# One transfer for each token tile's store, and single issues for the last pieces

## The chip, the cores and the metric

The kernel runs on one core of a Trainium2 chip. The metric is the device time of one execution in microseconds; the time of a kernel is the median of its runs.

## What is computed

Eight batches, twelve heads, 448 tokens, 64 values per head. Attention has no softmax: the scores are clipped at zero and squared. Its output, 3584 tokens of 768 values, goes through two weight matrices with a clipped square between them.

```python
scores = (q @ k.T) / sqrt(64)              # per batch and head, 448 x 448
attn   = maximum(scores, 0) ** 2 / 448
x      = (attn @ v), heads side by side    # 3584 x 768
h      = x @ w_in                          # 3584 x 2048
g      = maximum(h, 0) ** 2
out    = g @ w_out                         # 3584 x 768, float32
```

## The kernel before

Work goes by pairs of batches, `pr` = 0 to 3. For each pair there is a stage that forms g (batches 0 and 1 with plain products, line 430; later ones with a Strassen scheme, line 559) and then an output stage that forms `out` (line 746, seven half products for two token tiles, a Strassen scheme again). The attention of later batches is woven into both stages in `visit`s (lines 263 to 273, 329, 388).

**Token tiles.** The 448 tokens of a batch are laid out as 64 partitions times J = 7, token = 7p + j. A token tile of the output has 128 rows, that is two values of j with 64 partitions each; a pair of batches has seven such tiles, `tb` = 0 to 6. Tile 3 takes j = 6 of the first batch and j = 0 of the second; every other tile lies in one batch.

**Groups.** An output stage is a list of groups, each of two token tiles: `groups` in `o_steps`. Even pairs have three groups and save their tile 6; odd pairs have four, with the saved tile in the second. The last group of all is `LAST`, tiles 5 and 6 of pair 3. Within a group the products run in the order end1, end2, end6, end5, end7, end4, end3, each named for what happens after it: `end2` allocates the two output tiles `osb` and writes the first half row of the first of them (VectorE, line 653), `end4` finishes the second tile (ScalarE, line 696) and stores it, `end3` finishes the first tile (VectorE, line 653) and stores it. The first product of the next group is placed ahead of end4's.

**Output tiles.** `osb0` and `osb1` have two buffers each (pool "osb", 2). A buffer is written again two groups later, after its store has landed.

**Stores and queues.** `store` (lines 577 to 585) issues two transfers for each token tile, one for each j, from 64 partitions each. SyncE issues them. SyncE also issues the DMA transposes that turn q and k for the attention units to come (line 120); a unit's transposes are issued about two units ahead of its use. GpSimd issues the loads (lines 95 to 144); those of q and k for a later unit (line 109) reuse a buffer that the transposes read, and so wait for them.

**The last group** stores in pieces: two half rows on SyncE (end2, end7), a half row on GpSimd (end4), and the last half row in two quarters (`end3_part`), of which SyncE issues the first j and ScalarE the second:

```python
plus(0, c, "u5", acc=W, cc=cc)
store(rows[0], osb[0], c, nc.sync, nc.scalar)
```

Of the kernel before, what the change touches and what calls it, by code (L numbers as in the profile page):

```python
# [18 lines left out]
def kernel(  # L19
# [9 lines left out]
    nc = tc.nc  # L29

    B, H, S, D = q.shape
# [12 lines left out]
    J = 7  # L44
# [529 lines left out]
        return [(0.096, step(p, r, m), r == 0 and m == 0 and p not in (0, 1, 6, 8))  # L574
                for p in range(14) for r in range(2) for m in range(NH)]

    def store(row, osb, c, eng, eng2=None):
        pr, tb = row
        for i in range(2):
            b, j = divmod(2 * tb + i, J)  # L580
            b += 2 * pr
            (eng2 if eng2 and i else eng).dma_start(  # L582
                out=out[b * S:(b + 1) * S, :].rearrange(
                    "(p j) d -> p j d", j=J)[:, j, c],
                in_=osb[64 * i:64 * i + 64, c])
# [31 lines left out]
    def o_groups(groups, then):  # L617
# [5 lines left out]
        def group(n, rows, last):  # L623
# [3 lines left out]
            c0, c1 = slice(0, HALF), slice(HALF, DM)  # L627
# [8 lines left out]
            def ahead(i, k=n):  # L636
                if k < len(groups) and i not in sets[k]:
                    flush_g(needs(k))
                    sums(i, groups[k], sets[k])
# [11 lines left out]
            def plus(row, c, nm, acc=Y, cc=slice(0, HALF)):  # L651
                now_ve(0.5)
                nc.vector.scalar_tensor_tensor(  # L653
                    out=osb[row][:, c], in0=acc[0][:, 0:cc.stop - cc.start], scalar=CO,
                    in1=keep[nm][:, cc], op0=ALU.mult, op1=ALU.add)
# [8 lines left out]
            def end2():  # L664
                new_osb()
                plus(0, c0, "m1")
                if last:
                    store(rows[0], osb[0], c0, nc.sync)
# [8 lines left out]
            def end7():  # L677
                copy("u3")
                plus(1, c1, "u3")
                if last:  # L680
                    store(rows[1], osb[1], c1, nc.sync)
                    t = late["m"].tile([P, S], FP32, name="u5", tag="a")[:, 0:HALF]
                    nc.vector.scalar_tensor_tensor(
                        out=t, in0=Y[0][:, 0:HALF], scalar=CO, in1=keep["u2"],
                        op0=ALU.mult, op1=ALU.add)
                    keep["u5"] = t
# [4 lines left out]
            def end4():  # L691
                if last:
                    plus(1, c0, "u3", acc=Z)
                    store(rows[1], osb[1], c0, nc.gpsimd)
                    return
                nc.scalar.activation(out=osb[1][:, c0], in_=X[0][:, 0:HALF],
                                     func=AF.Copy, scale=CO)
                store(rows[1], osb[1], slice(0, DM), nc.sync)
                ahead(1, n + 1)
                ahead(2, n + 1)  # L700
# [5 lines left out]
            def end3_part(z):  # L706
                h = HALF // 2
                cc = slice(z * h, z * h + h)
                c = slice(HALF + cc.start, HALF + cc.stop)
                plus(0, c, "u5", acc=W, cc=cc)  # L710
                store(rows[0], osb[0], c, nc.sync, nc.scalar)

            products = (
                (X, True, lambda: tile_of(rows[0])[:, LO], b11, end1),
# [2 lines left out]
                (Y, True, lambda: ss[1], t1, end5),  # L717
                (X, False, lambda: ss[3], t3, end7),
                (X, False, lambda: tile_of(rows[1])[:, HI], nt4, end4),
                (Y, False, lambda: ss[4], b22, end3))  # L720

            def step3(z, f):
                h = HALF // 2

                def run():
                    if f == 0:
                        W[:] = [mm_tile(z)]
                    nc.tensor.matmul(
                        W[0][:, 0:h], lhsT=ss[4][:, f], rhs=b22[:, f, z * h:z * h + h],
                        start=(f == 0), stop=(f == KH - 1))  # L730
                    if f == KH - 1:
                        end3_part(z)
                return run
# [313 lines left out]
```

## Time and profile before

| | |
|---|---|
| median of 3 runs | 369.84 us (369.5 to 369.86) |
| the profiled execution | 369.71 us |
| its span | 367.9 us, granted TensorE clock 0.999 |
| busy share of the span | PE 98%, VectorE 72%, ScalarE 68%, GpSimd 29% |
| DMA | 42.65 MB moved, mean 116 GB/s |
| stores of 192 KB (SyncE) | 52, median 3.3 us from issue to landing |
| stores of the last group | 10: six of 96 KB and four of 48 KB, medians 2.2 to 2.9 us |

PE is TensorE's matmuls, DVE is VectorE, ACT ScalarE, POOL GpSimd, SP SyncE; a "q" behind a name is that engine's sequencer. The output stages lie at about 78 to 119, 162 to 212, 253 to 290 and 326 to 363 us of the span. Loads end at about 300 us; after that only stores move.

### The profile page before, as it was taken

The numbers are of one execution on the slowest core, as the hardware profiler recorded it, in microseconds if no ns is written. First come the engines' busy times: TensorE is split into PE (matmuls) and PEld (weight loads), VectorE is DVE, ScalarE is ACT, GpSimd is POOL, SyncE is SP. The second block draws the span as 40 slices with busy tenths as digits, with TensorE's granted clock in tenths as the row PEclk, the third lists the DMA queues.
The fourth block names the chain that finished last, engine by engine and source line by source line (L and its number), as shares of the span: only waits on it lengthen the run. The fifth ranks groups of instructions, "written<-read, shape, count | busy, mean of one in ns | idle before, by whom it ended". The sixth has DMA issues, their size and how long they took to land.

```text
span 367.9 us, 8740 instructions
## 1 busy us (share of the span) xinstructions
PE 358.8 (98%) x3588; PEld 232.1 (63%) x3588; DVE 265.3 (72%) x470; ACT 248.6 (68%) x384; POOL 107.2 (29%) x128
## 2 busy tenths in 40 slices
PE   8899999999999999999999999999999999999994
PEld 3644445445556788875555687886555689976662
DVE  2997677987867679888575667788876687784442
ACT  3988895788676998877655678886766785532220
POOL 8635521856552254531045225320000000000001
PEclk9999999999999999999999999999999999999999
DMA  8999999999999999967799998992323300003333
GB/s 119 196 204 203 205 204 161 144 160 166 207 124 155 170 111 134 99 92 61 138 146 125 156 159 83 107 90 52 67 71 87 86 3 2 2 0 87 86 96 78
DMA packets 121160, 42.65 MB, mean 116 GB/s; under 512 B 100832, under 2 KB 117760, under 8 KB 121120
## 3 DMA queue, kind: packets, MB, share of 16 engines
q0 software_dynamic: 82912, 23.01, 61.7%
q1 hardware_dynamic: 38048, 18.98, 26.5%
q8 instruction: 28, 0.46, 0.5%
q10 hardware_dynamic: 160, 0.10, 0.1%
q14 instruction: 12, 0.10, 0.1%
HBM read 45.61 MB, written 11.01 MB: 154 GB/s over the span
## 4 chain that ended last, share of the span: by engine, by line
PE 89%; DVE 4%; ACT 3%; issue 2%; DMA 1%; POOL 0%; POOLq 0%; ACTq 0%
PE mm L746 33%; PE mm L559 27%; PE mm L430 9%; PE slot L263 9%; PE slot L329 7%; ACT at L273 2%; DVE at L388 1%; DMA k<-in_k_dram 1%; DVE at L304 1%; PE mm L263 1%; PE avt L287 1%; PE slot L238 1%; ACT xt L342 1%; PE mm L238 0%; DVE osb L653 0%
## 5 line engine op out<-in xcount | busy, mean ns | idle before, releaser
L273 ACT ACTIVATE at<-slot 128x896 f16<-128x896 f32 x156 | 135.5, 927 | 7.4 <-PE slot L263 7.4
L388 DVE TENSOR_TENSOR at<-at 128x896 f16<-128x896 f16 x147 | 86.7, 618 | 12.6 <-ACT at L273 11.9
L109 POOL DMA_DIRECT2D qs<-in_q_dram x36 | 35.3, 983 | 111.1 <-DMA qT<-qs 102.8
L746 PEld LDWEIGHTS <-s 128*128 128x128 f16 x440 | 41.8, 98 | 32.2 <-issue 4.8
L559 PEld LDWEIGHTS <-w 128*128 128x128 f16 x576 | 53.8, 98 | 6.8 <-issue 6.0
L263 PE MATMUL slot<-qT,kT 64*64 64x448 f16 x696 | 53.2, 359 | 1.9 <-ACT at L273 1.4
L559 PE MATMUL mm<-xt,w 128*128 128x224 f16 x432 | 49.2, 259 | 0.0
L746 PEld LDWEIGHTS <-g 128*128 128x128 f16 x336 | 31.9, 98 | 23.5 <-issue 3.8
L559 PEld LDWEIGHTS <-ws 128*128 128x128 f16 x432 | 40.8, 98 | 2.8 <-issue 2.8
L746 PE MATMUL mm<-b,g 128*128 128x384 f16 x224 | 40.7, 326 | 0.0
L430 PE MATMUL mm<-xt,w 128*128 128x448 f16 x192 | 39.8, 354 | 0.0
L746 PE MATMUL mm<-b,s 128*128 128x384 f16 x216 | 39.5, 326 | 0.0
L746 PE MATMUL mm<-t,s 128*128 128x384 f16 x224 | 38.8, 326 | 0.0
L109 POOL DMA_DIRECT2D ks<-in_k_dram x36 | 35.2, 979 | 9.6 <-DMA b<-in_moe_w_out_dram 5.8
L263 PEld LDWEIGHTS <-kT 64*64 64x64 f16 x744 | 20.3, 104 | 27.6 <-issue 21.5
L653 DVE SCALAR_TENSOR_TENSOR osb<-mm,u 128x384 f32<-128x384 f32 (+1 forms) x30 | 16.2, 541 | 28.4 <-ACT u L648 20.9
L582 POOL DMA_DIRECT2D out_dram<-osb x2 | 1.1, 563 | 120.9 <-DVE osb L653 120.9
L502 DVE CUSTOM_DVE_ANT_0 g<-mm,m 128x448 f16<-128x448 f32 x36 | 22.4, 621 | 18.4 <-PE mm L559 7.8
L648 ACT ACTIVATE u<-mm 128x384 f32<-128x384 f32 x28 | 14.2, 507 | 30.5 <-PE mm L746 28.4
L559 PE MATMUL mm<-x,ws 128*128 128x224 f16 x288 | 33.7, 259 | 0.0
L329 PE MATMUL slot<-at,vt 64*64 64x448 f16 x560 | 30.1, 349 | 0.0
L430 PEld LDWEIGHTS <-w 128*128 128x128 f16 x192 | 17.1, 98 | 19.2 <-issue 5.1
(80 smaller groups left out, 417.2 us busy)
## 6 DMA issues: line engine op xcount, KB each, us to landing
out_dram<-osb SPq DMA_DIRECT2D x52, 192.0 KB, 3.3
vt<-in_v_dram POOLq DMA_DIRECT2D x24, 224.0 KB, 6.8
qs<-in_q_dram POOLq DMA_DIRECT2D x36, 112.0 KB, 4.9
ks<-in_k_dram POOLq DMA_DIRECT2D x36, 112.0 KB, 5.8
w<-in_moe_w_in_dram POOLq DMA_DIRECT2D x8, 384.0 KB, 12.1
b<-in_moe_w_out_dram POOLq DMA_DIRECT2D x4, 768.0 KB, 17.1
q<-in_q_dram POOLq DMA_DIRECT2D x6, 224.0 KB, 7.2
k<-in_k_dram POOLq DMA_DIRECT2D x6, 224.0 KB, 7.7
```

The source lines that it names most:

```text
L109: nc.gpsimd.dma_start(out=t[:, :, hh, :], in_=heads(src, n)[:, hh].rearrange("p (j d) -> p j d", d=D))
L238: nc.tensor.transpose(pss[i][64 * hh:64 * hh + 64, i if n < 4 else 0, j * P:(j + 1) * P], src[:, hh, j * D:(j + 1) * D], ident)
L263: nc.tensor.matmul(ps[hh][c, 0:S] if spare else ps[c, hh, 0:S], lhsT=kT[r, j, c], rhs=qT[r, :, c], start=True, stop=True)
L273: nc.scalar.activation(out=at, in_=ps[:, :, 0:S], func=AF.Relu, scale=SK)
L329: nc.tensor.matmul(ps[hp][64 * hh:64 * hh + 64, 0:S] if spare else ps[64 * hh:64 * hh + 64, hp, 0:S], lhsT=vt[r, hh, j * D:(j + 1) * D], r ...
L388: lambda: nc.vector.tensor_mul(at, at, at), 0))
L430: nc.tensor.matmul(cell[0][:, 0:S], lhsT=w1[f // 4][:, m, (f % 4) * P:(f % 4 + 1) * P], rhs=xts[b][:, m, :], start=(m == 0), stop=(m == NM ...
L502: nc.vector._custom_dve(TENSOR_ADD_SAT, out=gs(s, hi, right), in0=acc(s, y), in1=keep[s, nm], s0=3.4e38, s1=0.0)
L559: nc.tensor.matmul(XY[s][y][:, r * Q:(r + 1) * Q], lhsT=left(k, i0 + 2 * s + r, m), rhs=right(k, m), start=(fresh and r == 0 and m == 0), ...
L648: nc.scalar.activation(out=t, in_=X[0][:, 0:HALF], func=AF.Copy, scale=CO)
L653: nc.vector.scalar_tensor_tensor(out=osb[row][:, c], in0=acc[0][:, 0:cc.stop - cc.start], scalar=CO, in1=keep[nm][:, cc], op0=ALU.mult, op ...
L746: nc.tensor.matmul(acc[0][:, 0:HALF], lhsT=left()[:, f], rhs=right[:, f], start=(fresh and f == 0), stop=(f == KH - 1), skip_group_check=n ...
```

## The change

A token tile that lies in one batch is stored by one transfer of 128 partitions. Its destination is addressed as j, then partition, then column, with two values of j. A tile that lies in two batches (tb = 3) keeps its two transfers. `store` loses its second engine. In the last group the half row of `end4` is issued by ScalarE and not by GpSimd, and the two quarters of `end3_part` by ScalarE and SyncE, one each.

```diff
-    def store(row, osb, c, eng, eng2=None):
+    def store(row, osb, c, eng):
+
         pr, tb = row
+        b, j = divmod(2 * tb, J)
+        if j + 1 < J:
+            b += 2 * pr
+            eng.dma_start(
+                out=out[b * S:(b + 1) * S, :].rearrange(
+                    "(p j) d -> j p d", j=J)[j:j + 2, :, c],
+                in_=osb[:, c])
+            return
         for i in range(2):
             b, j = divmod(2 * tb + i, J)
             b += 2 * pr
-            (eng2 if eng2 and i else eng).dma_start(
+            eng.dma_start(
                 out=out[b * S:(b + 1) * S, :].rearrange(
                     "(p j) d -> p j d", j=J)[:, j, c],
                 in_=osb[64 * i:64 * i + 64, c])
...
-                    store(rows[1], osb[1], c0, nc.gpsimd)
+                    store(rows[1], osb[1], c0, nc.scalar)
...
-                store(rows[0], osb[0], c, nc.sync, nc.scalar)
+                store(rows[0], osb[0], c, (nc.scalar, nc.sync)[z])
```

## The prediction

> **What bounds the kernel now.** I read the chain that ended last first, then the stores' own rows, then the stretches in which only stores move.
>
> The chain's last pieces (start, length, what) are:
>
> ```profile
> 319.98 6.33 PE mm L559 x66
> 326.31 35.10 PE mm L746 x216
> 361.41 0.67 PE mm L728 x8
> 362.08 0.05 issue
> 362.13 0.35 DVE osb L653
> 362.49 0.03 issue
> 362.51 0.56 POOL out_dram L582
> 363.07 0.56 POOLq L1042
> ```
>
> TensorE sets the time without a break until 362.08. After it come one VectorE result, a store issue and the drain to 367.9. No store stands in the chain before the end: all are hidden under PE. The 1.81 us between the span (367.9) and the profiled execution (369.71) I leave as they are.
>
> The stores' rows (KB of one, median us from issue to landing), and who waits on POOL behind the transposes that share SP's queue with them:
>
> ```profile
> out_dram<-osb SPq DMA_DIRECT2D x52, 192.0 KB, 3.3
> out_dram<-osb SPq DMA_DIRECT2D x4, 96.0 KB, 2.2
> ...
> POOL qs L109 <- DMA qT<-qs: 102.8, 14, 16.1
> ```
>
> Next a stretch of one us in which only stores move; the last two numbers are the mean busy share of the 16 DMA engines and GB/s:
>
> ```profile
> core 0: us, PE busy (x) PEld busy (x) DVE busy (x) ACT busy (x) POOL busy (x), PEclk, DMA share, GB/s
> 356.00:357.00 1.00, 1.00 (x8) 0.59 (x6) 0.70 (x2) 0.00 (x0) 0.00 (x0) 1.00 0.98 280
> ```
>
> A mean share of 0.98 can only be read if all 16 engines work. One engine then moves 280 / (16 x 0.98) = 17.9 GB/s. The DMA view of 330 to 360 us has one slice at 307 GB/s, so 19.2 per engine at least are possible.
>
> Last, the room that the output buffers leave. VectorE writes each group's first half row of osb at:
>
> ```profile
> 338.10 0.56 DVE L653 SCALAR_TENSOR_TENSOR osb<-mm,m 128x384 f32<-128x384 f32 x1 [0.80 <-PE mm L746]
> ...
> 347.20 0.56 DVE L653 SCALAR_TENSOR_TENSOR osb<-mm,m 128x384 f32<-128x384 f32 x1 [0.80 <-PE mm L746]
> ```
>
> and SP issues a group's four stores at:
>
> ```profile
> 335.96 2.48 SPq L582 DMA_DIRECT2D out_dram<-osb  x4
> ...
> 345.06 2.48 SPq L582 DMA_DIRECT2D out_dram<-osb  x4
> ```
>
> A group takes 9.1 us here, and osb has two buffers a row. The stores of 335.96 to 338.44 must have landed by 347.2, when that buffer is written again: about 9 us of room, where 3 are used.
>
> [...] Now both sides of a store begin with 64, so k = 16; the share of 0.98 agrees. The new destination is written "j p d" and begins with j = 2 (steps: 768 elements for j, 5376 for p), while the source begins with 128[...]. No run shown has such a transfer. [...]
>
> **The change part by part.**
>
> *Issues.* Of 28 token tiles, the four with tb = 3 straddle two batches and stay as two stores. The other 24 are merged, two of them in pieces. Issues: 52 + 10 before, 22 + 5 + 8 = 35 after; SP goes from 58 to 33. At 0.58 us each that frees 25 x 0.58 = 14.5 us of SP, none on the chain before the end: nothing for the time.
>
> *The tail.* The last piece's two issues are at 363.15 (SP) and 363.44 (ACT, behind its issue of 362.51); one issue on SP at 363.15 ends 0.29 earlier. POOL's two issues (0.56 each) and its drain up to 366.8 go; SP's own drain stands at 366.5, so at most 0.3 more. Gain with 16 engines: 0.3 to 0.6 us. ACT has no compute left behind end4, so the issue moved to it delays nothing but its own next store.
>
> *The transfers.* This is the term that decides. A row tile has 128 x 768 x 4 = 393.2 KB. On 16 engines at 280 GB/s it needs 1.4 us. On two engines at 19.2 GB/s (38.4 together) it needs 10.24; a group of two, 20.5. A split row puts 1/8 of itself on these two engines: 1.28 us. Against 20.5 us stands a group period of 9.1 to 13 us, so the queue grows and the osb buffer, written two groups on, is late. The wait sits on VectorE (L653). Behind it are the sums and squares that PE needs and the accumulator that PE overwrites two products on; I give PE 0.5 us of cover. No one else hides it.
>
> I step through the four output stages: data starts 1.1 us after issue and closes 1.0 after its end (together 2.1, the shortest landing of a store in the trace); D is the accumulated delay.
>
> Stage 0: group 0's stores (93.7, 95.8) drain at 115.3 and close at 116.3; the buffer is wanted at 108.95 + 0.5: D = 6.8. Stage 1 (four groups): stores from 175.2 + 6.8 drain at 203.6, wanted at 189.4 + 0.5: D = 14.7; the second group drains at 224.1, wanted at 201.3 + 0.5: D = 23.3. Stage 2: drained 309.8, wanted 280.9 + 0.5: D = 29.4. Between stages the queue empties. Stage 3: first group drained 386.9, wanted 347.2 + 0.5: D = 40.2; second group 407.4, wanted 356.3 + 0.5: D = 51.6; third (one split row) 418.9. Only then the last two tiles, 2 x 10.24 us, whose pieces are all issued by then: 439.4. Closing 1.0 and the final barrier 1.4 (366.5 to 367.9): 441.8. That is 73.9 over 367.9; 369.71 + 73.9 = 443.6. The median of the runs shown is only 0.13 above that execution.
>
> *Transposes and loads.* [...] The one of 97.26 would land near 118; its first use is near 124.6. Those of 122 land near 150, used at 149.5 + D: cover just holds, since D moves the use too. POOL's loads wait for the transposes (the 102.8 us row) and share the two engines; I take nothing for it.
>
> *Bounds of the unknown.* Both unknowns lie in the two engines' rate. [...] At 17.3 (2.56 MB at a share of 30.8% over 30 us, the DMA view of 330 to 360) they give 458.8, so 461. Up to 302 us loads run too, and in 93 to 97 the engines' share reads 1.86: packets overlap. At 25 GB/s in stages 0 and 1, 30 in stage 2, it is 480.5 or 482; at half rate in three stages, 531. I take 19.2, the fastest that the trace shows. A gain has only the tail's 0.6 to come from.
>
> **Rivals.**
> 1. *k stays 16* (the access pattern is carried otherwise than I read it). For it: everything now shown is at 16 engines[...]. Against it: an order of elements in which j is not outermost would not match 128 consecutive partitions. Then the stores stay hidden and the tail gives 0.3 to 0.6: 369.2, no change. Chance 0.10.
> 2. *Faster.* With 16 engines, and POOL's drain (3.75 us from 363.06) being what the end waits for: its removal, plus the 0.29, decides if the close moves up by more than 0.74 us. SP's drain at 366.5 speaks against so much. 368.7; chance 0.04.
> 3. *Two engines, [...]*, so that osb is hardly late and mainly the last stage's backlog shows: 392 to 415. For it: four rows per engine and store, as now, may measure latency more than rate. Chance 0.22.
> 4. *Two engines, and the loads take their part of them* up to 302 us, so that transposes and stores fall behind further: 465 to 530. The 1.86 speaks for it. Chance 0.17.
>
> My case, 415 to 465, has 0.47.
>
> **How the numbers follow.** Slower is my case with 3 and 4: 0.86; same 0.10; faster 0.04. (A measurement here tells about 0.2%, 0.74 us, from no change.) The likeliest time is 444. The range for 8 in 10 leaves out the 0.14 at no change or faster and the outer ends: 386 to 505.
>
> **What would show it.** Right: row stores of 384 KB that land in 10 us alone and 20 to 50 in a queue; in 330 us and later a DMA share near 2/16 = 0.12, constant, at 35 to 60 GB/s; waits of DVE L653 for DMA out_dram; PE idle some 50 us in all; a last stretch without PE of some 20 us. Wrong: 384 KB stores landing in about 4 us and a chain that again ends with PE at 362. If the landing is 10 us and PE doesn't wait, the buffers' room is misread; if DVE doesn't wait but PE waits for qT, it is the transposes.

## The result, and the profile after

The changed kernel takes 440.44 us, median of 4 runs (436.4 to 443.75), against 369.85 before: 1.1873 times, interval 1.1788 to 1.1958. Ratios and intervals, here and below, leave out executions more than 1.5% longer than the shortest of the same kernel; medians are of all. The profiled execution took 439.55 us, its span is 437.8.

The page of the changed kernel, in part: busy times, and in 40 slices of 10.9 us the busy tenths of PE, the granted clock and the DMA engines.

```profile
span 437.8 us, 8701 instructions
...
PE 373.4 (85%) x3588; PEld 237.7 (54%) x3588; DVE 264.9 (61%) x470; ACT 249.5 (57%) x384; POOL 105.0 (24%) x126
...
PE   7999999999699809999767999499999999977640
...
PEclk9999999999899957999996999789999999996785
DMA  8999999999929969989499991997121100011211
...
out_dram<-osb SPq DMA_DIRECT2D x22, 384.0 KB
```

PE has holes in and after the first two output stages, and in the last stage up to the end. Its idle time is 437.8 - 373.4 = 64.4 us, 9.1 before: 55.3 of the 69.9 us by which the span grew. The other 14.6 are PE's own busy time, 373.4 in place of 358.8 for the same instructions: the row PEclk is below 9 only where the row PE has a hole or just behind one, and on the page the 128x384 matmuls of `t` and `s` take 354 ns on average, 326 before.

The chain of the changed kernel from 368 us on (start, length, what):

```profile
368.77 19.52 PE mm L755 x120
...
388.90 22.53 DMA out_dram<-osb
...
411.56 0.57 DVE osb L662
...
412.17 6.97 PE mm L755 x24
...
420.50 0.36 DVE osb L662
```

Before, PE ran through the last stage for 35.10 us without a break. Now it runs for 19.52, and then a store leads: VectorE wants the output buffer of two groups ago and waits for its transfer. In the whole execution such waits, and those of PE, sum to (us, times, longest):

```profile
DVE osb L662 <- DMA out_dram<-osb: 35.8, 6, 9.6
...
PE mm L755 <- DVE osb L662: 24.3, 6, 7.4
...
PE slot L263 <- DMA kT<-ks: 12.2, 2, 11.9
...
PE slot L263 <- issue: 6.2, 1, 6.2
```

PE stands 24.3 us behind VectorE's output buffers and 12.2 us before scores whose transposed k hasn't landed; for 6.2 us more, before scores too, the profile names nothing that ended the wait.

A stretch after the last matmul, with stores only (share of the 16 DMA engines and GB/s last):

```profile
422.00:430.00 8.00, 0.00 (x0) 0.00 (x0) 0.00 (x0) 0.00 (x0) 0.00 (x0) 0.68 0.13 50
```

0.13 x 16 = 2.1: the work of two engines, at 25 GB/s each, as the prediction took it (its k is the number of engines that carry one transfer). That a destination that begins with 2 gets two was not shown ahead of this run. In the line of before the share was 0.98 and the rate 280 GB/s.

The transposes in SP's queue, the changed kernel:

```profile
93.52 2.58 SPq L583 DMA_DIRECT2D out_dram<-osb  x2
96.40 12.19 SPq L120 DMA_TRANSPOSE qT<-qs  x1
108.69 3.18 SPq L120 DMA_TRANSPOSE kT<-ks  x1
...
138.02 15.61 SPq L120 DMA_TRANSPOSE qT<-qs  x1
153.73 3.45 SPq L120 DMA_TRANSPOSE kT<-ks  x1
```

The transpose of q that was issued in 1.49 us at 97.26 before now holds SP for 12.19 us, a later one for 15.61. The stores of the next group stand behind it, and so do POOL's loads, which wait for it (152.6 us in all, 102.8 before).

### The profile page after: what moved, and what is told of

The parts are those of the page before. It is cut to its first block, busy times and chain, and to the rows that moved or that the text cites. A ratio compares the mean times of both kernels' runs of the same rounds, so it can differ in the third digit from the quotient of the medians.

```text
span 437.8 us, 8701 instructions
## 1 busy us (share of the span) xinstructions
PE 373.4 (85%) x3588; PEld 237.7 (54%) x3588; DVE 264.9 (61%) x470; ACT 249.5 (57%) x384; POOL 105.0 (24%) x126
## 4 chain that ended last, share of the span: by engine, by line
PE 58%; DMA 27%; DVE 5%; issue 3%; ACT 2%; SPq 0%; POOL 0%; DVEq 0%; ACTq 0%; POOLq 0%
PE mm L559 22%; DMA out_dram<-osb 21%; PE mm L755 16%; PE mm L430 8%; PE slot L263 6%; DMA kT<-ks 5%; PE slot L329 5%; ACT at L273 2%; DVE osb L662 1%; DVE at L388 1%; DMA k<-in_k_dram 1%; DVE at L304 1%; PE avt L287 1%; SPq L120 0%; PE slot L238 0%
## 5 line engine op out<-in xcount | busy, mean ns | idle before, releaser
L273 ACT ACTIVATE at<-slot 128x896 f16<-128x896 f32 x156 | 135.5, 925 | 25.5 <-PE slot L263 25.4
L755 PEld LDWEIGHTS <-s 128*128 128x128 f16 x440 | 44.3, 103 | 62.1 <-issue 37.7
L109 POOL DMA_DIRECT2D qs<-in_q_dram x36 | 35.1, 978 | 159.8 <-DMA qT<-qs 152.6
L263 PE MATMUL slot<-qT,kT 64*64 64x448 f16 x696 | 54.3, 362 | 20.4 <-DMA kT<-ks 12.2
L755 PE MATMUL mm<-t,s 128*128 128x384 f16 x224 | 44.8, 354 | 24.3 <-DVE osb L662 24.3
L559 PEld LDWEIGHTS <-w 128*128 128x128 f16 x576 | 55.5, 101 | 8.3 <-issue 6.5
L559 PE MATMUL mm<-xt,w 128*128 128x224 f16 x432 | 51.5, 267 | 0.0
L559 PEld LDWEIGHTS <-ws 128*128 128x128 f16 x432 | 42.0, 101 | 4.3 <-issue 3.5
L755 PE MATMUL mm<-b,s 128*128 128x384 f16 x216 | 42.7, 344 | 0.0
L559 PE MATMUL mm<-x,ws 128*128 128x224 f16 x288 | 35.9, 269 | 0.5 <-issue 0.5
L662 DVE SCALAR_TENSOR_TENSOR osb<-mm,m 128x384 f32<-128x384 f32 x14 | 7.8, 557 | 42.7 <-DMA out_dram<-osb 35.8
L508 DVE TENSOR_TENSOR g<-g 128x896 f16<-128x896 f16 x48 | 28.7, 619 | 0.4 <-ACT g L511 0.4
## 6 DMA issues: line engine op xcount, KB each, us to landing
w<-in_moe_w_in_dram POOLq DMA_DIRECT2D x8, 384.0 KB, 11.9
```

The lines of the kernel that those rows point to most:

```text
L109: nc.gpsimd.dma_start(out=t[:, :, hh, :], in_=heads(src, n)[:, hh].rearrange("p (j d) -> p j d", d=D))
L263: nc.tensor.matmul(ps[hh][c, 0:S] if spare else ps[c, hh, 0:S], lhsT=kT[r, j, c], rhs=qT[r, :, c], start=True, stop=True)
L273: nc.scalar.activation(out=at, in_=ps[:, :, 0:S], func=AF.Relu, scale=SK)
L508: lambda: nc.vector.tensor_mul(g, g, g), b))
L559: nc.tensor.matmul(XY[s][y][:, r * Q:(r + 1) * Q], lhsT=left(k, i0 + 2 * s + r, m), rhs=right(k, m), start=(fresh and r == 0 and m == 0), ...
L662: nc.vector.scalar_tensor_tensor(out=osb[row][:, c], in0=acc[0][:, 0:cc.stop - cc.start], scalar=CO, in1=keep[nm][:, cc], op0=ALU.mult, op ...
```

## Experiments

**Where the number of engines is taken away.** e1 addresses the destination as partition, then j, so that it begins with 64 and not with 2:

```diff
-                    "(p j) d -> j p d", j=J)[j:j + 2, :, c],
+                    "(p j) d -> p j d", j=J)[:, j:j + 2, c],
```

> As the changed kernel, but the destination of a merged store is addressed as partition, then j, then column[...]; the two rows of a partition pair land in another order within a token tile, bytes and issues are the same. Theory A (two engines carry a merged store, the backlog is the cost): 369.2 to 369.8 us, stores of 384 KB land in some 4 us, DMA share near 0.9 where only stores move. Rival B (the single large transfer is what costs: one semaphore for 128 rows, larger waits): over 400 us. If the tail's single issues are worth something it shows here as up to 0.6 us under 369.85.

Measured: 368.7 us, 0.9964 times before (0.9953 to 0.9975). Its 384 KB stores land in 2.9 us, and two stretches of one us in its last stage read

```profile
355.00:356.00 1.00, 1.00 (x9) 0.60 (x7) 0.28 (x1) 0.00 (x0) 0.00 (x0) 1.00 0.84 341
357.00:358.00 1.00, 1.00 (x8) 0.61 (x7) 0.84 (x2) 0.49 (x1) 0.00 (x0) 1.00 0.95 260
```

So the single transfer, its size and its semaphore cost nothing; all 71 us belong to the destination's first dimension of 2. Rival B falls. (e1 puts rows in another order, so it is a test and not a version to use. Two neighbouring rows of 3 KB also become one run of 6 KB in it; but the stores of before had runs of 3 KB and kept all 16 engines busy (a share of 0.98), so that isn't what counts.) Worked out as in the prediction, one engine's rate is 341 / (16 x 0.84) = 25.4 GB/s in the first line and 260 / (16 x 0.95) = 17.1 in the second: such short stretches don't give one figure.

**The last group alone, and all but the last group.** e2 has merged stores in the last group only; e3 everywhere else, with before's queues at the end.

```diff
-        if j + 1 < J:
+        if j + 1 < J and row in LAST:        # e2
+        if j + 1 < J and row not in LAST:    # e3
```

> Merged stores only in the last group (with the changed kernel's queues); all other stores are two of 64 rows. Theory A: 786 KB on two engines at 50 GB/s (the rate that the changed kernel shows at its end) from 356.9 on: drained near 374, so 378 us in all, 8.5 over before; PE busy to 362 as before. Rival B: as A, or less, near 371, since only five transfers are concerned.

> Merged stores everywhere but in the last group, whose ten half stores and queues are those of before. Theory A: the stalls of PE stay, and of the changed kernel's end (17.3 us after the last matmul, 5.8 before) most goes: 428 to 434 us. If the last group's backlog were the main cost: near 390.

Measured: e2 380.16 us (1.0266, 1.0237 to 1.0295), e3 424.26 (1.1457, 1.1419 to 1.1495). The last group is worth 10 us, the middle 54; together 64 of the 71, so the two parts add up nearly. e2 lies 2 us over what was expected; e3 4 under the lower end.

**Half the bytes on the two engines.** e4 merges only tiles with an even tb, and the last group.

```diff
-        if j + 1 < J:
+        if j + 1 < J and (tb % 2 == 0 or row in LAST):
```

> Only tiles with even tb are merged (and the last group), so that most groups have one merged and one split tile: two engines get 393 x 1.125 = 442 KB in place of 786 for a group, 8.8 us at 50 GB/s against a period of 9.1 to 13 us. Theory A (a queue that saturates): almost all stalls of the middle go, only the end's 8 to 10 us and a few us from the one group with two merged tiles stay: 378 to 388 us. Rival B, or a cost for each merged store: half of the middle's cost stays, 400 to 410.

Measured: 411.92 us (1.1099, 1.105 to 1.1148). That refutes theory A as it stood: with half the bytes more than half of the cost is still there, just over the rival's 400 to 410. Either a merged store has a cost of its own, or a queue that isn't saturated hurts in another way than by buffers. The next runs look for that.

**The last stage alone.** e9 merges only in stage 3, where nothing else moves.

```diff
-        if j + 1 < J:
+        if j + 1 < J and (pr == 3 or row == (2, 6)):
```

> Merged stores in the last output stage only (pr = 3 and the saved tile in it), where no loads and no transposes run. Theory A (the prediction's steps of buffer and queue, with the rate of 50 GB/s that the changed kernel shows there): the buffers are late by 6.1 and 12.8 us, the queue ends at 393.1, so 397 us. With the prediction's 38.4 GB/s it would be 414. Rival (a merged store costs more than its time on two engines): over 405.

Measured: 397.09 us (1.0739, 1.072 to 1.0757). VectorE's first writes of groups 2 and 3 in e9, with what they waited for in brackets:

```profile
354.09 0.56 DVE L662 SCALAR_TENSOR_TENSOR osb<-mm,m 128x384 f32<-128x384 f32 x1 [7.67 <-DMA out_dram<-osb]
369.17 0.56 DVE L662 SCALAR_TENSOR_TENSOR osb<-mm,m 128x384 f32<-128x384 f32 x1 [5.91 <-DMA out_dram<-osb]
```

Before they stood at 347.20 and 356.30. They are late by 6.9 and 12.9 us; the steps of buffer and queue at 50 GB/s gave 6.1 and 12.8, and 397 for the end. In this stage, then, buffer and queue account for the whole cost, to within 1 us at each buffer. The rival's 405 and the 414 of the prediction's rate are refuted.

**The first stage, with and without a buffer that waits.** e10 merges in stage 0 only; e11 leaves its first group unmerged.

```diff
-        if j + 1 < J:
+        if j + 1 < J and pr == 0 and tb < 6:        # e10
+        if j + 1 < J and pr == 0 and 1 < tb < 6:    # e11
```

> Merged stores in the first output stage only (five tiles), where loads and transposes run. In the changed kernel the delay at the end of this stage's influence is 20.0 us (first write of osb in the next stage at 186.5 in place of 166.6). Theory A (buffer and queue alone, 50 GB/s): 2.1 us of delay, 372. Theory B (transposes and loads of the next units wait for the two engines, and that is the middle's cost): 386 to 391.

> As e10_stage0 without the first group: tiles 2, 4 and 5 of pair 0 are merged, so that no group writes a buffer whose merged store is still under way. Theory A: no delay, 370. Theory B: the transposes behind these three stores (1.18 MB, 23.6 us of two engines) still come late: 378 to 388.

Measured: e10 388.18 us (1.0498, 1.0468 to 1.0528), e11 375.66 (1.0156, 1.0128 to 1.0184). e10 is in theory B's range. That range came from the changed kernel's own delay of 20.0 us, so it shows that stage 0's stores alone bring this delay; what carries it the traces of e10 and e11 have to show. e11 lies between the two theories, 2 us under B's range. In e11's trace VectorE waits for no store; its chain shows what does lead:

```profile
138.27 2.42 PE mm L559 x24
141.34 10.78 DMA kT<-ks
152.54 2.98 PE mm L559 x30
```

and SP's queue what came ahead of that:

```profile
121.14 2.77 SPq L583 DMA_DIRECT2D out_dram<-osb  x2
124.08 17.15 SPq L120 DMA_TRANSPOSE qT<-qs  x1
141.34 3.45 SPq L120 DMA_TRANSPOSE kT<-ks  x1
```

Two merged stores, then a transpose of q that takes 17.15 us to issue, then the one of k, which lands only near 152 and which PE needs. So late transposes are a cost of their own: 6.1 us with three merged stores. e10's first two merged stores bring another 12.5 us: the buffer is late by 6.2 (its third first-write stands at 115.11, 108.95 before), and the next unit's kT leads the chain for 9.93 us.

**Another queue for the stores.** e5 issues the merged whole tiles from ScalarE, e8 from GpSimd.

```diff
-                store(rows[1], osb[1], slice(0, DM), nc.sync)
+                store(rows[1], osb[1], slice(0, DM), nc.scalar)    # e5; nc.gpsimd in e8
...
-                store(rows[0], osb[0], slice(0, DM), nc.sync)
+                store(rows[0], osb[0], slice(0, DM), nc.scalar)    # e5; nc.gpsimd in e8
```

> The changed kernel with its 22 merged whole-tile stores issued by ScalarE and not SyncE; they keep their two engines. In the changed kernel SP's transposes of q took 8 to 15.6 us to issue behind a store (1.2 before), and loads and scores wait for them. Theory A1 (SP's own queue is what holds the transposes): on ACT's queue they issue in 1.2 to 3 us again, the waits of DVE for osb (36 us in all) stay, total 395 to 418 us. Rival A2 (whatever the queue, the transposes are late because they need the same two engines, busy with stores): transposes land as late as now, 430 to 445. If ACT itself is held at its issues, PE stalls at scores and the time goes over 440.

> The changed kernel with its 22 merged whole-tile stores issued by GpSimd; destination as in the changed kernel[...]. [...] stores land in 8 to 12 us, SP's transposes issue in 1.2 to 3 us, osb is nearly always ready: 385 to 395 us, of which some 8 to 15 come from the last group and from GpSimd's loads that now stand in one queue with stores. If GpSimd always takes the same two engines: 425 to 450 as the changed kernel.

Measured: e5 429.46 us (1.1601, 1.1569 to 1.1632). SP's row for the transposes of q, minimum, median and longest, e5 and then the changed kernel:

```profile
L120 SPq DMA_TRANSPOSE qT<-qs x18: 1221/1223/6183, 60.3 to 290.6; - x18
```

```profile
L120 SPq DMA_TRANSPOSE qT<-qs x18: 1222/1282/15607, 60.5 to 301.8; - x18
```

SyncE is rid of the longest holds. Of PE's waits shown for the changed kernel, e5 keeps only the one behind VectorE's output buffers, and that has grown:

```profile
PE mm L755 <- DVE osb L662: 30.5, 5, 9.1
```

For a transpose PE waits nowhere in e5 by as much as 0.5 us (the waits with no named end are at most 1.9 us each, at the scores' weight loads). So A2 doesn't hold, though 429 lies next to its range: off the stores' queue the transposes come in time, and it was SyncE's own queue that made them late for PE, as A1 says. A1's time is missed by 11 us, because VectorE now waits longer for the buffers than the 36 us that it counted on (41.7 us); ScalarE, too, is held at a store's issue now and then, for up to 4.8 us. The gain is 11 us of 71: part of what PE no longer loses at the transposes it loses at the stores, which are no faster: from the start of VectorE's last write to the end 18.2 us pass (410.3 to 428.5), 17.3 in the changed kernel.

e8: 401.53 us, median of four executions from 392.1 to 407.21; 1.0653 times before (1.0606 to 1.0701), that is some 394 us, at the upper end of what was expected if GpSimd's stores don't all take the same two engines (385 to 395). Its trace is of an execution of 407.05 us. In the last stage there the line reads

```profile
360.00:370.00 10.00, 8.44 (x52) 4.98 (x51) 2.41 (x4) 1.96 (x4) 1.59 (x2) 1.00 0.32 87
```

87 GB/s and 0.32 x 16 = 5.1 engines: more than two work at a time, so the transfers that GpSimd issues don't all take the same two. Its stores wait in GpSimd's queue among the loads, and in this execution a store lands in 12.5 us (median) and osb still waits, for 27.7 us. e8 changes two things at once: it takes the stores out of SyncE's queue, which alone was worth 11 us in e5, and it spreads them over more engines. That the spreading brings most of the rest is likely; it wasn't separated from the change of queue.

**The tail.** e7 is the kernel before with end4's two stores on ScalarE and not on GpSimd.

```diff
-                    store(rows[1], osb[1], c0, nc.gpsimd)
+                    store(rows[1], osb[1], c0, nc.scalar)
```

> The kernel before with one change: end4's two half stores of the last group are issued by ScalarE in place of GpSimd. e1_k16_all gained 1.2 us; this tells what of it was GpSimd's issue and drain. If the end waits for GpSimd's drain: 369.0 to 369.3. If the single issues made the gain, ACT's three or four issues in a row (0.55 us each) cost here: 369.8 to 370.6.

Measured: 369.65 us, 0.9993 (0.9984 to 1.0003): no difference, and a time between the two that were expected. Taking GpSimd's issue and drain away gains nothing by itself. Whether ScalarE's added issues cost as much as the drain gave, e7 can't tell.

**A version with fast single stores and the output in order.** If x comes in the natural order of tokens, a token tile is 128 neighbouring rows. e6 gets the order from the scores' moving operand, e12 from the copy of x out of PSUM; in both, every tile is one store, also tb = 3.

```diff
-                    lhsT=kT[r, j, c], rhs=qT[r, :, c],
+                    lhsT=kT[r, j, c], rhs=qT[r, :, c].rearrange("k j p -> k p j"),    # e6
...
-            out=xts[b][:, 2 * u:2 * u + 2, :], in_=ps[:, :, 0:S],
+            out=xts[b][:, 2 * u:2 * u + 2, :].rearrange("p h (q j) -> p h q j", j=J),    # e12
+            in_=ps[:, :, 0:S].rearrange("p h (j q) -> p h q j", j=J),
...
+        r0 = 2 * pr * S + tb * P
+        eng.dma_start(out=out[r0:r0 + P, c], in_=osb[:, c])
```

> Scores read q in the order p, then j (the moving operand's columns with steps of 128 elements), so that x, g and osb come in the natural order of tokens: every token tile, tb = 3 too, is one store of 128 neighbouring rows, with the queues of the changed kernel; the output is complete and in order. If the moving operand's steps cost TensorE nothing: as e1_k16_all, 368.5 us, scores at 346 to 360 ns each. Rival: strided reads slow the 744 score matmuls, each by up to double (350 ns more)[...], and over 380 us in any case.

> Natural order of tokens by another place: x is put in order (partition, then j) where it is copied out of PSUM (lines 342, 338, and x0), 24 units; every token tile is one store of 128 neighbouring rows[...], with the queues of the changed kernel, and the output is complete and in order. If ScalarE reads PSUM with steps at the same speed (0.92 us a copy of 896 columns): 368.5 us as e1_k16_all. Rival: the copies slow down to double (0.9 us more, 21 times), some of it in PE's way: 370 to 380.

Measured: e6 467.36 us (1.2632, 1.2612 to 1.2652). Its scores, columns as in the groups of the page:

```profile
L263 PE MATMUL slot<-qT,kT 64*64 64x448 f16 x696 | 148.4, 922 | 0.1
```

and before

```profile
L263 PE MATMUL slot<-qT,kT 64*64 64x448 f16 x696 | 53.2, 359 | 1.9 <-ACT at L273 1.4
```

One takes 922 ns on average against 359. e12: 368.62 us, 0.9971 (0.996 to 0.9981), 0.3% less than before with an interval clear of 1, and 72 us less than the changed kernel. Its main copy of x, next to that of before:

```profile
L345 ACT ACTIVATE xt<-slot 128x896 f16<-128x896 f32 x20 | 18.3, 917 | 7.6 <-PE slot L333 7.5
```

```profile
L342 ACT ACTIVATE xt<-slot 128x896 f16<-128x896 f32 x20 | 18.3, 917 | 7.6 <-PE slot L329 7.5
```

The same 917 ns; the eight smaller copies of x, five of them on VectorE, keep their times too, within 2 ns. Its 384 KB stores land in 3.1 us (median). In e12 the span ends 3.4 us after the last VectorE result (363.20 + 0.36 to 367.0); before it was 4.8 (362.77 + 0.36 to 367.9). Its last pieces land in 1.8 to 1.9 us, before in 2.2 to 2.9: one transfer where there were two.

## Why the prediction was right, and where it wasn't

444 was forecast, 440.4 measured. The likeliest case is the one that came, but two of its terms were wrong by over 30 us each, in opposite directions. That they nearly cancel is luck: the part of the mechanism that concerns stores and buffers was right, the closeness of the number says little for the rest.

**k = 2: right.** Where the destination begins with 2 the share is 0.13, 2.1 engines; where it begins with 64 it is 0.98 before, and 0.84 and 0.95 in e1, 13 to 16 engines. The two carry the stores from SyncE and from ScalarE alike: from 425 to 433 us of the changed kernel SyncE's queue has 6.7% of the 16 engines and ScalarE's 6.6%, again 2.1 engines together. Of the stores from GpSimd more than two engines are busy, 5.1 in e8's line.

**The buffer and the queue: right.** The step through the last stage, with the measured rate, gave 397 for e9, which took 397.09; its two buffers came 0.8 and 0.1 us later than in the step. VectorE waits for out_dram in the changed kernel in six places, 35.8 us in all, and PE stands behind it for 24.3.

**The rate of one engine: too low.** The step took 19.2 GB/s, "the fastest that the trace shows". It is 25 in the changed kernel where nothing else moves, for 8 us on end. Short bursts on 16 engines, from which I read 17.9 and 19.2, are no measure of that: e1's two lines give 25.4 and 17.1. Why bursts differ so is not shown. With 50 GB/s for the pair the prediction's own steps give 407.7, not 443.6: 35.9 us too many.

**"I take nothing" for transposes and loads: too little.** This is the step that failed. It let SyncE go on issuing while transposes waited on the two engines (a wait that no run had shown), and had them land at 118 and 150, in time for their use. In the changed kernel the issue itself is held, 8 to 15.6 us for each of seven transposes of q, and the next ones are issued later. The third transpose of q after stage 0's first stores stood at 122.13 before and stands at 138.02; its k follows at 153.73 in place of 123.85, and PE waits 11.9 us for that k. While SyncE is held, the stores and loads behind it slip as well. VectorE's first write of osb in stages 1 to 3, and the end of the span:

| | before | after | late by | forecast | steps at 50 GB/s |
|---|---|---|---|---|---|
| stage 1 | 166.56 | 186.52 | 20.0 | 6.8 | 2.1 |
| stage 2 | 256.81 | 298.69 | 41.9 | 23.3 | 9.0 |
| stage 3 | 329.10 | 371.56 | 42.5 | 29.4 | 10.4 |
| end | 367.9 | 437.8 | 69.9 | 73.9 | 38.0 |

From stage 3's first write to the end, where only stores move, 27.4 us are added; the steps at 50 GB/s say 27.6. Up to stage 3 it is 42.5 and not 10.4: 32 us that buffers and queue at this rate don't explain.

Where the delay is added tells two kinds apart. Inside stages 0 to 2, from a stage's first such write to its last, 18.3 us are added, where VectorE waits for a buffer. Between a stage's last such write and the first of the next stage 24.1 us are added, where the prediction put nothing. In e5, with the stores out of SyncE's queue, the two are 28.1 and 5.0. So most of the 24.1 is SyncE held at its transposes, and e11 shows that cost alone, 6 us with no store waited for. The 8 us by which the first kind exceeds the steps go with a slower pair of engines: in e10 the first group's 786 KB took some 19.4 us, 40 GB/s, while loads and transposes moved too. That these slow it is likely and not shown; no run takes the loads away.

**PE's clock: not in the prediction.** 14.6 us of the 69.9 are PE's own slower work. They lie within the delays of the table, of both kinds and of the end, and aren't one more cause beside them.

**The tail: right in sign, too small.** 0.3 to 0.6 us were forecast for 16 engines; e1 and e12 gain 1.3 and 1.1. Half of the forecast was GpSimd's drain, which by itself gains nothing (e7). Single pieces land sooner: the two last quarters in 2.5 us in e1 and in 1.9 in e12, in 2.7 and 2.9 before, and SyncE's own drain ends at 365.8 in e1, at 366.5 before. How the rest of the gain divides is open. In the changed kernel none of it can show: its tail is 17.3 us (420.50 to 437.8) in place of 5.1 from the same point.

**The rivals.** With 16 engines "no change, 369.2" would have been slightly off and "faster, 368.7" would have hit; whether by the drain is open. Rival 3, two engines at a higher rate, was nearer: 407.7 lies in its range, whose lower end, 392, rested on a rate that no run shows. Rival 4 had transposes and stores falling behind further, though by the loads and not by SyncE's queue. What came is both together.

## What to carry to other kernels

When two transfers are merged into one, look at the first dimension of the destination: here one that begins with 2 put a 384 KB store on two engines, and cost 71 us where the same bytes, begun with 64 partitions, gained 1.3. A transfer that is hidden has a rate that it needs and a buffer that says until when; if the rate falls, here from 280 GB/s to 50, price not only that buffer but also what is issued behind it from the same queue, here transposes and, behind them, more stores and loads. Another queue freed the transposes (e5), but the stores got no faster, and it gave back 11 us of 71. And where an order stands in the way of a better transfer, look for the operation that can change it for nothing: a PSUM copy on ScalarE did, a matmul's moving operand did not.

## What the runs showed of the hardware that was not expected

- A matmul whose moving operand (64 x 448, fp16) steps by 128 elements takes 922 ns on average in place of 359 (e6): 2.6 times.
- ScalarE's copy of 896 columns out of PSUM takes 917 ns whether it reads them in order or with steps of 64 elements (e12).
- TensorE's granted clock was lower where PE idled between stretches of work: in e9 it is 0.66 from 350 to 360 us, where PE is busy for 5.29 of 10 us, and 1.00 in the ten before, with 8.44:

```profile
340.00:350.00 10.00, 8.44 (x52) 4.96 (x51) 2.40 (x4) 1.96 (x4) 0.00 (x0) 1.00 0.13 52
350.00:360.00 10.00, 5.29 (x25) 2.84 (x25) 2.37 (x5) 0.49 (x1) 0.00 (x0) 0.66 0.13 52
```

- A DMA transpose behind merged stores holds SyncE for up to 17.15 us at its issue (e11), where a transpose of q took 1.2 to 2.7 before; the merged stores themselves are mostly issued in 0.54 us (median, changed kernel). With the stores issued by ScalarE instead, SyncE's transposes of q take 1.22 us (median, e5), at most 6.18.
